# Expert slots without GpSimd arithmetic, weight splits two pieces at a time, and a first slot table that is good for eight slots

## The chip, the cores and the metric

The kernel runs on one core of one Trainium2 chip, which has eight. A core has a matrix engine (PE, TensorE), a vector engine (DVE, VectorE), a scalar engine (ACT, ScalarE), GpSimd (POOL) and SyncE (SP), which here only issues transfers. They run their own instruction streams in order and wait for each other on semaphores. The metric is the device time of one execution in microseconds (us); the lower one is better.

## The reference

The program is an attention with packed keys, a dense two-layer network, and a network of eight experts of which each token takes one:

```
x = attention(q, attention(p, k, v))        # 8 x 8 heads, 576 tokens, width 64; p packs to 32
x: 4608 tokens x 512                         # heads put side by side
h = x @ w_in                                 # 512 -> 2048
g = where(h >= 1, h, where(h <= -1, 0, (h + 1)^2 / 4))
y = g @ w_out                                # 2048 -> 512
logits = y @ w_gate                          # 8 experts
e = argmax(logits); p = softmax(logits)[e]
out = p * (relu(y @ w1[e]) @ w2[e])          # 512 -> 1024 -> 512, the one expert of the token
```

All inputs are float32. With the inputs used, 4594 of the 4608 tokens take expert 2 and 14 take expert 3; the kernel does not know this when it is built.

## The kernel before

**Precision.** Each float32 operand of a product is split in two parts: `hi`, a rounded copy that PE takes at full rate, and `lo = raw - hi`. A product is three matmuls: hi*hi, hi*lo, lo*hi. So each operand costs one copy (on ACT, as a rule) and one subtraction with two inputs in the on-chip memory (on DVE or POOL).

**Stages.** The attention and the packing of the weights take the first stretch. Then the dense network goes through the tokens in 12 tiles of 16 steps (`FC = 16`). A step computes 128 of the 2048 hidden features: the products `h` (L707), the activation on ACT (L729, L730), DVE (L731), ACT (`gh`, L736), DVE or POOL (`gl`, L737), and one step later the products `y` (L712 to L714). Beside tile t + 1 the finished rows of tile t are gated: 24 dot products of a 128x512 block with one expert's gate vector (`jk`, L515, one DVE instruction each with two inputs in the on-chip memory, and one more that reads the sum), then `route` (L517 on: largest logit, place of the token, and an indirect transfer by POOL that sends the row to its expert's list in DRAM). For each pair of blocks these are 8 items of two dots and one `route`.

Then 18 slots of 256 tokens follow, each for one expert, in 8 steps: `gh`, 12 matmuls (L877); `ggh` on ACT (L881) and `ggl` on DVE (L882); `gy`, 6 matmuls (L712 to L714). Last comes a half slot for what is left over. The program is built for any distribution of the tokens, so a **slot table** (`make_table`) is computed on the chip from the counts: which expert each slot takes, from which row on, and whether its weights have to be loaded anew. Table A serves the first `EARLY` slots from the counts known by then, table B the others from all counts. SP reads their entries into registers and issues the loads under a condition.

**Weights of a slot.** Four transfers bring 1 MB each (`raw0` to `raw3`, L825). Each is cut in 128x512 pieces: ACT copies (L860), and `lo_engine` says who subtracts (L861): POOL for all of slots 0 and 1 and half of slot 2, DVE afterwards. All 16 pieces are split for every slot, the weights loaded anew or not. The slot's tokens come as `xb`, are transposed on DVE (L843), copied by ACT (L844), and POOL makes their `lo` part (L845, 128x1024).

**What sets the order.** Everything beside the products is put on a list by step: `at(step, fn)`. Tiles have the steps 0 to 191, slot s starts at `GE + 8*s` with `GE = 192`. Within that, a scheduler at build time orders each engine's instructions, all engines but SP, whose order is that of the program. Tile 11 starts at step `base_a = 176`. Table A takes its counts at `base_a - FC`, that is at the start of tile 10, and is computed from there; the weights of slot 0 are loaded and split beside tile 11. The last tile's gates stand at steps `GE + m//3`, table B at `GE + 8`, and the constants of both tables (`index_tables`) at the start of tile 11.

Of the kernel before, what the change touches and what calls it, by code (L numbers as in the profile page):

```python
# [35 lines left out]
EARLY = 4  # L36
# [48 lines left out]
def attn_moe_kernel(ctx, tc, qT, kT, vv, pT, wcat, wg, w2cat, out):  # L85
# [481 lines left out]
    def index_tables(pl):  # L567


        NM = NMIN - EARLY  # L570
        k = {}
        pi = pl.tile([P, 2], I32, name="pi")
        pool.iota(pi, pattern=[[-1, 2]], base=0, channel_multiplier=1)
        ti = pl.tile([P, 2], I32, name="tail_i")
        dve.tensor_scalar(out=ti, in0=pi, scalar1=-float(NM), scalar2=0.0, op0=ALU.add, op1=ALU.max)
        hi = pl.tile([P, 2, 2], I32, name="half_i")
        dve.tensor_single_scalar(out=hi[:, 0], in_=ti, scalar=1, op=ALU.arith_shift_right)
        dve.tensor_single_scalar(out=hi[:, 1], in_=ti, scalar=1, op=ALU.bitwise_and)
        for n in ("p", "tail", "kf", "off", "cap"):
            k[n] = pl.tile([P, 2], F32, name="k_" + n)  # L580
        hf = pl.tile([P, 2, 2], F32, name="half_f")
        dve.tensor_copy(hf, hi)
        dve.tensor_copy(k["p"], pi)
        dve.tensor_copy(k["kf"], ti)
        dve.tensor_tensor(out=k["kf"], in0=k["p"], in1=k["kf"], op=ALU.subtract)
        dve.tensor_tensor(out=k["kf"], in0=k["kf"], in1=hf[:, 0], op=ALU.add)
        dve.tensor_scalar(out=k["off"], in0=hf[:, 1], scalar1=float(HS), scalar2=None, op0=ALU.mult)
        dve.tensor_scalar(out=k["tail"], in0=k["p"], scalar1=float(NM), scalar2=None, op0=ALU.is_ge)
        dve.tensor_scalar(out=k["cap"], in0=k["tail"], scalar1=float(SL - HS), scalar2=-float(SL), op0=ALU.mult, op1=ALU.add)
        tri8 = pl.tile([P, E, E], F32, name="tri8")  # L590
        pool.memset(tri8, 0.0)
        for e in range(E):
            pool.memset(tri8[:, e, 0:e + 1], 1.0)
        k["tri"] = tri8
        return k

    def make_table(sums, used, nm):
# [5 lines left out]
        k = p3[1]  # L603
# [92 lines left out]
        return ti, un  # L696
# [62 lines left out]
    def evac_tile(t):  # L759
# [198 lines left out]
    for n in range(FC2):  # L958
# [143 lines left out]
```

## Time and profile before

| | |
|---|---|
| three runs | 1266.15, 1267.1, 1267.31 us; median 1267.1 us |
| the profiled execution | 1269.05 us, of which the span of the instructions is 1267.3 us |
| busy share of the span | PE 95%, PEld 79%, DVE 75%, ACT 59%, POOL 33% |
| granted clock of PE, mean | 0.984 |
| tile 10 / tile 11 | 717.29 to 761.29 / 761.29 to 817.90 us |
| slots 0, 1, 2, 3 start at | 817.90, 846.90, 878.27, 904.18 us |
| slots 4 to 16 | 927.65 to 1222.61 us |

A tile's or slot's start is the start of its first product (`h`, L707, or `gh`, L877). PE is the engine that is busy nearly always, so the profile is read for the places where it isn't: how long a stage takes beside what its matmuls need, which wait lies in the gap, and what held the instruction that is waited for.

### The profile page before, as it was taken

What the parts mean: (1) busy time and instruction counts of PE and PEld (TensorE: products, weight loads), DVE (VectorE), ACT (ScalarE), POOL (GpSimd) and SP (SyncE); (2) the same over time, 40 slices, a digit from 0 to 9 for tenths busy, and PEclk for the clock granted to TensorE, in tenths of its full rate; (3) what the DMA queues carried; (4) which work ended last, traced back from release to release, by engine and by line L of the source; (5) the groups of instructions that cost most, each with busy time, mean ns of one, the idle gap of its engine ahead of it and who ended that gap; (6) DMA issues with size and microseconds to landing.
All of it is one profiled execution on the core that took longest, in us unless ns stands there. A gap on an engine that the chain in (4) does not pass through costs nothing.

```text
span 1267.3 us, 21548 instructions
## 1 busy us (share of the span) xinstructions
PE 1199.4 (95%) x7234; PEld 995.6 (79%) x7234; DVE 948.8 (75%) x2296; ACT 741.4 (59%) x1574; POOL 418.5 (33%) x618
## 2 busy tenths in 40 slices
PE   5769999999999999999999998988999999999997
PEld 2446888787788887688888877777899899999996
DVE  7787858988887869969679499798765666666663
ACT  5666656666665566566565556544555565565653
POOL 4230117524730217631113276677212122121210
PEclk8997999999999999999999999899999999999999
DMA  9994870153111232112331005102611212112150
GB/s 343 370 347 152 304 205 22 45 181 114 58 39 44 94 108 76 59 34 67 128 100 33 25 17 179 38 1 68 191 35 42 60 34 68 34 42 60 34 176 21
DMA packets 70183, 128.22 MB, mean 101 GB/s; under 512 B 10281, under 2 KB 46633, under 8 KB 66864
## 3 DMA queue, kind: packets, MB, share of 16 engines
q1 hardware_dynamic: 56464, 97.33, 23.8%
q0 software_dynamic: 5840, 18.95, 3.9%
q10 hardware_dynamic: 7760, 10.49, 2.7%
q8 instruction: 59, 0.97, 0.3%
q14 instruction: 60, 0.49, 0.1%
HBM read 162.31 MB, written 31.77 MB: 153 GB/s over the span
## 4 chain that ended last, share of the span: by engine, by line
PE 71%; DVE 17%; issue 4%; ACT 3%; DMA 3%; POOL 2%; SPq 0%; ACTq 0%; POOLq 0%; DVEq 0%
PE gh L877 14%; PE h L707 13%; PE y L712 8%; PE y L714 8%; PE y L713 8%; DVE jk L515 7%; PE gy L714 5%; PE gy L713 4%; PE gy L712 4%; PE pp L329 2%; DVE rt L731 1%; PE s L215 1%; PE sc L381 1%; PE pp L316 1%; DVE sw L861 1%
## 5 line engine op out<-in xcount | busy, mean ns | idle before, releaser
L707 PE MATMUL h<-ah,pw 128*128 128x256 f32 (+1 forms) x1024 | 243.3, 302 | 8.7 <-DVE rt L731 8.2
L877 PEld LDWEIGHTS gh<-gx,sw 128*128 128x128 f32 x1728 | 230.1, 192 | 14.3
L515 DVE CUSTOM_DVE_ANT_0 jk<-yr,wgb 128x512 bf16<-128x512 f32 x288 | 233.6, 811 | 5.6 <-ACT yr L764 3.5
L877 PE MATMUL gh<-gx,sw 128*128 128x256 f32 x1728 | 233.8, 283 | 0.0
L712 PE MATMUL y<-wo,gh 128*128 128x512 f32 x576 | 230.4, 400 | 0.3 <-ACT kp L391 0.3
L861 DVE TENSOR_TENSOR sw<-raw,sw 128x512 fp32r<-128x512 f32 x264 | 174.5, 710 | 73.1 <-ACT sw L860 73.0
L713 PE MATMUL y<-wo,gh 128*128 128x512 f32 x576 | 228.5, 397 | 0.0
L860 ACT CAST sw<-raw 128x512 fp32r<-128x512 f32 x304 | 169.5, 617 | 63.5 <-PE gy L714 56.1
L707 PEld LDWEIGHTS h<-ah,pw 128*128 128x128 f32 x1024 | 176.9, 190 | 32.7 <-DVE rt L731 14.9
L714 PE MATMUL y<-wo,gl 128*128 128x512 f32 x576 | 186.4, 401 | 2.6 <-POOL gl L737 2.5
L729 ACT ACTIVATE rt<-h,half 128x320 f32<-128x320 f32 (+1 forms) x192 | 111.1, 580 | 99.3 <-PE h L707 80.0
L736 ACT CAST gh<-rt 128x512 fp32r<-128x512 f32 (+2 forms) x192 | 98.2, 512 | 105.7 <-DVE rt L731 59.6
L707 PE MATMUL h<-al,pw 128*128 128x256 f32 (+1 forms) x512 | 152.8, 298 | 0.3 <-POOL al L236 0.3
L731 DVE SCALAR_TENSOR_TENSOR rt<-h,rt 128x320 f32<-128x320 f32 (+1 forms) x192 | 105.3, 550 | 53.2 <-ACT rt L730 48.5
L714 PEld LDWEIGHTS y<-wo,gl 128*128 128x128 f32 x576 | 105.6, 189 | 31.3 <-POOL gl L737 6.5
L712 PEld LDWEIGHTS y<-wo,gh 128*128 128x128 f32 x576 | 108.9, 189 | 25.7 <-issue 3.9
L713 PEld LDWEIGHTS y<-wo,gh 128*128 128x128 f32 x576 | 109.2, 190 | 18.6
L845 POOL TENSOR_TENSOR gx<-xT,gx 128x1024 fp32r<-128x1024 f32 (+1 forms) x19 | 45.6, 2398 | 235.3 <-ACT gx L844 220.2
L712 PE MATMUL gy<-sw,ggh 128*128 128x512 f32 x288 | 113.9, 396 | 0.2 <-ACT ggh L881 0.2
L713 PE MATMUL gy<-sw,ggh 128*128 128x512 f32 x288 | 114.0, 396 | 0.0
L881 ACT ACTIVATE ggh<-gh 128x256 fp32r<-128x256 f32 x144 | 54.9, 381 | 97.7 <-PE gh L877 94.6
L737 DVE TENSOR_TENSOR gl<-rt,gh 128x512 fp32r<-128x512 f32 (+1 forms) x128 | 89.2, 697 | 27.3 <-ACT gh L736 21.9
(220 smaller groups left out, 1827.1 us busy)
## 6 DMA issues: line engine op xcount, KB each, us to landing
raw<-in_w2cat SPq DMA_DIRECT2D x76, 1024.0 KB
ws<-wsd SPq DMA_DIRECT2D x48, 512.0 KB
wr<-in_wcat SPq DMA_DIRECT2D x16, 1024.0 KB
kp<-in_kT SPq DMA_DIRECT2D x16, 576.0 KB
xb<-xs SPq DMA_DIRECT2D x72, 128.0 KB
vr<-in_vv SPq DMA_DIRECT2D x16, 512.0 KB
wsd<-ws SPq DMA_DIRECT2D x8, 1024.0 KB
qr<-in_qT ACTq DMA_DIRECT2D x16, 320.0 KB
```

The source lines that it names most:

```text
L515: dve.tensor_tensor_reduce(out=junk, in0=rows[j][:, :DM], in1=wgb[0][:, e, :], scale=1.0, scalar=0.0, op0=ALU.mult, op1=ALU.add, accum_out ...
L707: pe.matmul(ps[:, col0:col0 + n], lhsT=w[:, g, part, c], rhs=x[:, g, col0:col0 + n], start=(n_mm == 0), stop=(n_mm == 5))
L712: pe.matmul(y, lhsT=gh, rhs=wh, start=first, stop=False)
L713: pe.matmul(y, lhsT=gh, rhs=wl, start=False, stop=False)
L714: pe.matmul(y, lhsT=gl, rhs=wh, start=False, stop=last)
L729: act.activation(v, ps[:, :W], AF.Relu, bias=half, scale=0.5)
L731: dve.scalar_tensor_tensor(out=v, in0=ps[:, :W], scalar=1.0, in1=v, op0=ALU.max, op1=ALU.min)
L736: act.copy(gh[:, :n], vk[:, :n])
L737: (pool if k == "A" else dve).tensor_tensor(out=gl[:, :n], in0=vk[:, :n], in1=f32(gh[:, :n]), op=ALU.subtract)
L860: act.copy(w[:, 0, :], r)
L861: lo_engine(sid, i, n).tensor_tensor(out=w[:, 1, :], in0=r, in1=f32(w[:, 0, :]), op=ALU.subtract)
L877: pe.matmul(ps[:, :SL], lhsT=first(sid, 4 * (fc // 4) + k, part)[:, c], rhs=rh[:, k, :], start=(n_mm == 0), stop=(n_mm == 3 * KD - 1))
```

## The change

- **Who subtracts.** The weight split is called by pair (`m` = 0 to 3) in place of by piece. From slot 1 on, ACT copies and DVE subtracts 128x2x512 in one instruction, and POOL takes none. Slot 0 keeps single pieces; POOL does those of the second layer (`i = 1`, eight), DVE those of the first. The tokens' `lo` part goes from POOL to DVE in two halves of 128x512.
- **The first table.** `EARLY` goes from 4 to 8: table A serves slots 0 to 7 and takes its counts one tile later, at `base_a`. Only three slots' registers are read at once, those of slots 3 to 7 when they are prefetched.
- **The constants** of the tables are made at the program's start.
- **The last tile's gates** stand at steps `GE + 3*m`, and table B is a generator that makes one of ten pieces a step, from `GE + 43` to `GE + 52`.

```diff
-EARLY = 4
+EARLY = 8
...
+    slot_index = index_tables(const)
...
-            at(FC * (t + 1) + (m // 3 if t == NTILE - 1 else min(m, 14 * m // (len(its) - 1))), it)
+            at(FC * (t + 1) + (3 * m if t == NTILE - 1 else min(m, 14 * m // (len(its) - 1))), it)
...
-        pool.tensor_tensor(out=xl[:, :, :W], in0=xT[:, :, :W], in1=f32(xh[:, :, :W]), op=ALU.subtract)
+        for k in range(0, KD, 2):
+            dve.tensor_tensor(out=xl[:, k:k + 2, :W], in0=xT[:, k:k + 2, :W], in1=f32(xh[:, k:k + 2, :W]), op=ALU.subtract)
...
-    def lo_engine(sid, i, n):
-
-        return pool if sid < 2 or (sid == 2 and i == 1) else dve
...
+    def split_w(sid, i, m):
+        w = wtile(f"wo{m}" if i else f"pw1{m}", [P, 2, 2, 512], F32R, f"sw{sid}_{i}_{m}")
+        slot[sid].setdefault("w", {})[i, m] = w
+        for n in (range(2) if sid == 0 else (slice(0, 2),)):
+            r = raw[m][:, n, 512 * i:512 * i + 512]
+            act.copy(w[:, n, 0], r)
+            (pool if sid == 0 and i else dve).tensor_tensor(out=w[:, n, 1], in0=r, in1=f32(w[:, n, 0]), op=ALU.subtract)
...
-        tabA[0], tabA[1] = make_table(sumsA[0], None, "A")
-        for i in range(EARLY):
+        for _ in make_table(sumsA[0], None, "A", tabA):
+            pass
+        for i in range(3):
             slot_regs(i, tabA[0], i, i > 0)
...
-    at(base_a - FC, lambda: sumsA.append(mcum[0]))
+    at(base_a, lambda: sumsA.append(mcum[0]))
...
-    for n in range(FC2):
-        at(base_a + (5, 6, 8, 9, 12, 13, 16, 17)[n], lambda n=n: split_w(0, 0, n))
-        at(base_a + 8 + n, lambda n=n: split_w(0, 1, n))
+    for m in range(4):
+        at(base_a + (6, 9, 13, 17)[m], lambda m=m: split_w(0, 0, m))
+        at(base_a + 9 + 2 * m, lambda m=m: split_w(0, 1, m))
...
-    at(GE + 8, phase_b)
+    for n in range(10):
+        at(GE + 43 + n, phase_b)
...
-        for n in range(FC2):
-            at(b0 + 3 + n, lambda nx=nx, n=n: split_w(nx, 0, n))
-            at(b0 + 2 + n, lambda nx=nx, n=n: split_w(nx, 1, n))
+        for m in range(4):
+            at(b0 + (3, 5, 7, 9)[m], lambda nx=nx, m=m: split_w(nx, 0, m))
+            at(b0 + 2 + 2 * m, lambda nx=nx, m=m: split_w(nx, 1, m))
```

The first place is ACT beside tile 11, from its fifth step's activation (`rt180`) on; `sw0_i_n` is a piece of slot 0's weights of layer `i`. Before:

```order
L729 ACTIVATE rt180_8887<-h11_4_8878,half_94 128x320
L730 ACTIVATE rt180_8887<-rt180_8887 128x320
L729 ACTIVATE rt181_8918<-h11_5_8909,half_94 128x320
L730 ACTIVATE rt181_8918<-rt181_8918 128x320
L736 CAST gh180_8885<-rt180_8887 128x384
L860 CAST sw0_0_0_8936<-raw0_8841 128x512 x2
L860 CAST sw0_1_0_9049<-raw0_8841 128x512 x2
L736 CAST gh181_8916<-rt181_8918 128x384
L729 ACTIVATE rt182_8952<-h11_6_8943,half_94 128x320
L730 ACTIVATE rt182_8952<-rt182_8952 128x320
L860 CAST sw0_1_2_9148<-raw1_8872 128x512 x2
L736 CAST gh182_8950<-rt182_8952 128x384
```

The same place now, five steps further on:

```order
L740 ACTIVATE rt186_9105<-h11_10_9096,half_94 128x320
L741 ACTIVATE rt186_9105<-rt186_9105 128x320
L867 CAST sw0_0_0_8938<-raw0_8814 128x512 x2
L867 CAST sw0_1_0_9086<-raw0_8814 128x512 x2
L747 CAST gh186_9103<-rt186_9105 128x384
L867 CAST sw0_0_1_9091<-raw1_8845 128x512 x2
L867 CAST sw0_1_1_9146<-raw1_8845 128x512 x2
L740 ACTIVATE rt187_9130<-h11_11_9121,half_94 128x320
L740 ACTIVATE rt188_9160<-h11_12_9151,half_94 128x320
L741 ACTIVATE rt187_9130<-rt187_9130 128x320
L867 CAST sw0_0_2_9210<-raw2_8876 128x512 x2
L867 CAST sw0_1_2_9215<-raw2_8876 128x512
```

The first copy of slot 0's weights moved from behind the sixth step's activation to behind the eleventh's, and eight copies stand there within two steps.

The second place is DVE in slot 0, between its third and fourth `ggl` (`ggl0_2`, `ggl0_3`) and on; `jk11_j_e` are the last tile's dots, `sw1` the next slot's weights. Before:

```order
L882 SCALAR_TENSOR_TENSOR ggl0_2_9412<-gh0_2_9398,ggh0_2_9411 128x256
L515 ISA jk11_0_6_9386,L11_0_9316<-yr11_0_9310,wgb_1712 128x512
L515 ISA L11_0_9316 128x1
L515 ISA jk11_0_7_9388,L11_0_9316<-yr11_0_9310,wgb_1712 128x512
...
L882 SCALAR_TENSOR_TENSOR ggl0_3_9486<-gh0_3_9472,ggh0_3_9485 128x256
L515 ISA jk11_1_0_9390,L11_0_9316<-yr11_1_9312,wgb_1712 128x512
...
L532 MAX mx811_0_0_9433<-L11_0_9316 128x8
L515 ISA jk11_1_1_9392,L11_0_9316<-yr11_1_9312,wgb_1712 128x512
```

And now:

```order
L890 SCALAR_TENSOR_TENSOR ggl0_2_9367<-gh0_2_9353,ggh0_2_9366 128x256
L547 ISA jk11_0_6_9584,L11_0_9290<-yr11_0_9284,wgb_1743 128x512
L547 ISA L11_0_9290 128x1
L869 TENSOR_TENSOR sw1_1_0_9377<-raw0_8814,sw1_1_0_9377 128x2x512
L890 SCALAR_TENSOR_TENSOR ggl0_3_9394<-gh0_3_9380,ggh0_3_9393 128x256
L547 ISA jk11_0_7_9586,L11_0_9290<-yr11_0_9284,wgb_1743 128x512
...
L869 TENSOR_TENSOR sw1_0_1_9460<-raw1_8845,sw1_0_1_9460 128x2x512
L890 SCALAR_TENSOR_TENSOR ggl0_4_9424<-gh0_4_9410,ggh0_4_9423 128x256
L547 ISA jk11_1_0_9677,L11_0_9290<-yr11_1_9286,wgb_1743 128x512
```

Between two `ggl` there are now one dot and one subtraction of 128x2x512 where two or three dots stood; the dots of slot 0 are still 16.

## Rows read from the trace of the kernel before

**Rows 1.** Windows by stage: tile 10, tile 11, slots 0 to 3, slots 4 to 16.

```profile
core 0: us, PE busy (x) PEld busy (x) DVE busy (x) ACT busy (x) POOL busy (x), PEclk, DMA share, GB/s
717.29:761.29 44.00, 42.59 (x214) 34.11 (x212) 36.59 (x126) 24.64 (x57) 29.75 (x52) 1.00 0.05 19
761.29:817.90 56.61, 50.57 (x239) 42.19 (x239) 46.39 (x123) 33.28 (x70) 37.23 (x48) 0.94 0.43 122
817.90:927.65 109.75, 98.25 (x594) 85.24 (x593) 92.25 (x211) 53.69 (x112) 60.30 (x45) 0.98 0.24 75
927.65:1222.61 294.96, 294.66 (x1874) 266.56 (x1873) 184.45 (x365) 175.16 (x352) 56.90 (x39) 1.00 0.18 54
```

**Rows 2.** Start, length: products of tile 11's last steps, as one step begins and the next.

```profile
811.94 0.31 PE L707 MATMUL h<-ah,pw 128*128 128x320 f32 x1
...
814.92 0.31 PE L707 MATMUL h<-ah,pw 128*128 128x320 f32 x1
```

**Rows 3.** PE's waits (us in total, times, longest): tile 11, then slots 0 to 3.

```profile
PE h L707 <- DVE rt L731: 3.8, 3, 2.3
PE rk L544 <- DVE M L537: 2.2, 1, 2.2
...
PE gy L714 <- DVE ggl L882: 10.0, 8, 2.1
```

**Rows 4.** Window of ten us behind tile 11's waits.

```profile
790.00:800.00 10.00, 6.25 (x21) 5.21 (x22) 8.22 (x17) 3.34 (x8) 7.14 (x10) 0.71 0.70 104
```

**Rows 5.** Timeline of PE in slot 1.

```profile
852.14 1.11 PE L714 MATMUL gy<-sw,ggl 128*128 128x512 f32 x2 [2.10 <-DVE ggl L882]
```

**Rows 6.** Timeline of DVE: a dot in tile 10; in slot 1 a dot, a `ggl`, a small one.

```profile
753.86 0.68 DVE L515 CUSTOM_DVE_ANT_0 jk<-yr,wgb 128x512 bf16<-128x512 f32 x1
...
848.25 1.81 DVE L515 CUSTOM_DVE_ANT_0 jk<-yr,wgb 128x512 bf16<-128x512 f32 x1
...
851.67 0.41 DVE L882 SCALAR_TENSOR_TENSOR ggl<-gh,ggh 128x256 fp32r<-128x256 f32 x1
...
876.96 3.16 DVE L657 TENSOR_TENSOR eefB<-eefB,eehB 128x2 f32<-128x2 f32 x1
```

**Rows 7.** Timeline of POOL beside slot 1's dots.

```profile
848.23 2.96 POOL L861 TENSOR_TENSOR sw<-raw,sw 128x512 fp32r<-128x512 f32 x2
```

**Rows 8.** Groups by line (busy, mean ns of one, idle before) in slots 0 to 3.

```profile
L861 DVE TENSOR_TENSOR sw<-raw,sw 128x512 fp32r<-128x512 f32 x36 | 29.9, 870 | 7.4 <-ACT sw L860 7.3
L515 DVE CUSTOM_DVE_ANT_0 jk<-yr,wgb 128x512 bf16<-128x512 f32 x24 | 28.8, 1198 | 0.3
...
L861 POOL TENSOR_TENSOR sw<-raw,sw 128x512 fp32r<-128x512 f32 x26 | 38.5, 1508 | 7.3 <-ACT sw L860 7.1
```

**Rows 9.** Groups of the whole run and of slots 4 to 16: pieces, pairs.

```profile
L289 DVE TENSOR_TENSOR ws<-ca,ws 128x1024 fp32r<-128x1024 f32 x8 | 10.1, 1259 | 1.6 <-ACT ws L288 1.6
...
L861 DVE TENSOR_TENSOR sw<-raw,sw 128x512 fp32r<-128x512 f32 x209 | 132.6, 685 | 58.8 <-ACT sw L860 58.8
...
L844 ACT CAST gx<-xT 128x1024 fp32r<-128x1024 f32 x13 | 13.7, 1054 | 0.0
```

**Rows 10.** Timelines of DVE, POOL, SP, ACT: table A and slot 0's weights.

```profile
752.31 0.15 DVE L626 SCALAR_TENSOR_TENSOR cA<-iota,cnA 128x8 f32<-128x8 f32 x1
...
766.82 0.72 POOL L541 TENSOR_TENSOR mcum<-mcum,M 128x8 f16<-128x8 f16 x2 [0.97 <-DVE M L537]
...
767.12 0.16 DVE L689 CAST tiA<-tfA 128x4 int32<-128x4 f32 x1
...
774.44 2.30 SPq L825 DMA_DIRECT2D raw<-in_w2cat  x4
...
779.62 2.19 ACT L860 CAST sw<-raw 128x512 fp32r<-128x512 f32 x4 [1.80 <-DMA raw<-in_w2cat]
...
783.97 1.14 ACT L860 CAST sw<-raw 128x512 fp32r<-128x512 f32 x2 [0.82 <-DMA raw<-in_w2cat]
```

**Rows 11.** Timeline of DVE in the first stretch.

```profile
7.70 0.76 DVE L388 TENSOR_REDUCE nm<-sc 128x1 f32<-128x576 f32 x1 [2.96 <-PE sc L381]
```

More of the change, by code (lines that the diff above doesn't have):

```diff
@@ L127, in attn_moe_kernel, with index_tables @@
                 pool.iota(tokid[:, t, j:j + 1], pattern=[[0, 1]], base=t0 + tile_start(t) + c - (HB if tile_kind(t) == "B" else 0), channel_multiplier=1)
+    def index_tables(pl):
+        NM = NMIN - EARLY
+        k = {}
+        pi = pl.tile([P, 2], I32, name="pi")
+        pool.iota(pi, pattern=[[-1, 2]], base=0, channel_multiplier=1)
+        ti = pl.tile([P, 2], I32, name="tail_i")
+        dve.tensor_scalar(out=ti, in0=pi, scalar1=-float(NM), scalar2=0.0, op0=ALU.add, op1=ALU.max)
+        hi = pl.tile([P, 2, 2], I32, name="half_i")
+        dve.tensor_single_scalar(out=hi[:, 0], in_=ti, scalar=1, op=ALU.arith_shift_right)
+        dve.tensor_single_scalar(out=hi[:, 1], in_=ti, scalar=1, op=ALU.bitwise_and)
+        for n in ("p", "tail", "kf", "off", "cap"):
+            k[n] = pl.tile([P, 2], F32, name="k_" + n)
+        hf = pl.tile([P, 2, 2], F32, name="half_f")
+        dve.tensor_copy(hf, hi)
+        dve.tensor_copy(k["p"], pi)
+        dve.tensor_copy(k["kf"], ti)
+        dve.tensor_tensor(out=k["kf"], in0=k["p"], in1=k["kf"], op=ALU.subtract)
+        dve.tensor_tensor(out=k["kf"], in0=k["kf"], in1=hf[:, 0], op=ALU.add)
+        dve.tensor_scalar(out=k["off"], in0=hf[:, 1], scalar1=float(HS), scalar2=None, op0=ALU.mult)
+        dve.tensor_scalar(out=k["tail"], in0=k["p"], scalar1=float(NM), scalar2=None, op0=ALU.is_ge)
+        dve.tensor_scalar(out=k["cap"], in0=k["tail"], scalar1=float(SL - HS), scalar2=-float(SL), op0=ALU.mult, op1=ALU.add)
+        tri8 = pl.tile([P, E, E], F32, name="tri8")
+        pool.memset(tri8, 0.0)
+        for e in range(E):
+            pool.memset(tri8[:, e, 0:e + 1], 1.0)
+        k["tri"] = tri8
+        return k
+    slot_index = index_tables(const)
     packed = st2.tile([P, 2 * B, D], F32, name="packed")
@@ L565, in gate_items, with make_table @@
         return items
[L567 to L603, printed above, removed]
+    def make_table(sums, used, nm, out_tab):
+        k = slot_index
         def t(shape, dt, n):
@@ L638, in make_table @@
         if used is not None:
+            yield
             nh = t([P, E], F32, "nh")
@@ L666, in make_table @@
         dot(c, oh, 1)
+        yield
         j = t([P, 1], F32, "j")
@@ L695, in make_table @@
             dve.scalar_tensor_tensor(out=un, in0=Sf, scalar=float(EARLY), in1=un, op0=ALU.min, op1=ALU.subtract)
-        return ti, un
+        out_tab.extend((ti, un))
     def ffn1(t, fc, ps):
@@ L957, in attn_moe_kernel, with phase_b @@
     at(base_a + 13, lambda: slot_x(0))
[L958 to L960 removed]
+    for m in range(4):
+        at(base_a + (6, 9, 13, 17)[m], lambda m=m: split_w(0, 0, m))
+        at(base_a + 9 + 2 * m, lambda m=m: split_w(0, 1, m))
     nact = [None]
[L964 to L966 removed]
+    def phase_b(box=[]):
+        if not box:
+            box.append(make_table(mcum[0], tabA[1], "B", tabB))
+        next(box[0], None)
     def count_slots():
         nact[0] = nc.values_load(tabB[0][0:1, 3:4], min_val=0, max_val=NTAIL, skip_runtime_bounds_check_because="halves left of NT tokens")
[L971 removed]
     at(GE + FC2 * (NMIN - 2), count_slots)
[L973 removed]
+    for n in range(10):
+        at(GE + 43 + n, phase_b)
     def regs_for(sid):
[L976 removed]
+        if 2 < sid < EARLY:
+            slot_regs(sid, tabA[0], sid, True)
+        elif sid >= EARLY:
             slot_regs(sid, tabB[0], sid - EARLY, sid > EARLY, SL if sid < NMIN else HS)
@@ L1049, in attn_moe_kernel @@
                 slot_x(sid)
-                for n in range(FC2):
-                    split_w(sid, 0, n)
-                    split_w(sid, 1, n)
+                for m in range(4):
+                    split_w(sid, 0, m)
+                    split_w(sid, 1, m)
             half_slot(sid)
```

26 lines of the change are left out of this document (9 added, 17 removed).

## The prediction, made before the changed kernel ran

> **What bounds the kernel now.** I read the windows by stage first, to see where PE is not full. Slots 4 to 16 take 294.96 us and PE is busy 294.66 of them [rows 1]: 22.69 us a slot, the products alone. Slots 0 to 3 run the same products and take 109.75, which is 18.99 over 4 x 22.69. Tile 11's last `y` products fall behind slot 0's first product; nine of 512 columns beside six of 320 are 0.71 of a step, and a step without a wait takes 814.92 - 811.94 = 2.98 us [rows 2], so 2.1 of the 18.99 are work. 16.9 us are lost. Tile 11 needs 16 x 2.98 = 47.7 and takes 56.61: 8.9 lost.
>
> The second view is PE's list of waits. In tile 11, 3.8 us stand with `rt` and 2.2 with `M` [rows 3], 6.0 in all. The rest is the clock: in the ten us behind these waits, in which PE was busy for 6.25, the granted clock is 0.71 [rows 4], so nearly six of ten at the lower of the two levels (1.2 in place of 2.4 GHz), about 2.9 lost; 6.0 + 2.9 = 8.9. In slots 0 to 3 10.0 of the lost 16.9 stand with `ggl`, eight times [rows 3].
>
> The third is DVE's timeline ahead of such a wait. PE begins at 852.14 after 2.10 us for `ggl` [rows 5]; that `ggl` takes 0.41, begins at 851.67 and stands behind two dots, of which the first took 1.81 [rows 6]. A dot in tile 10 took 0.68. POOL ran its splits beside the slow ones [rows 7]. Over the four slots 24 dots mean 1198 ns, POOL's 26 splits 1508 [rows 8]; and a subtraction of two columns took 3.16 [rows 6]. So DVE instructions with two inputs in the on-chip memory and POOL's splits lengthen each other, and DVE, busy 92.25 of 109.75 [rows 1], delivers `ggl` late.
>
> **Slots 0 to 3.** POOL's 26 splits go. The 24 dots return to about 0.69: 24 x (1.198 - 0.69) = 12.2 us of DVE time. All splits then are DVE's: 62 pieces are 31 pairs. A pair is not in the trace as such; the nearest rows are the 128x1024 subtraction, 1259 ns, and two pieces at 2 x 685 = 1370 [rows 9]. I take the first, the same element count in one instruction: 31 x 1.26 = 39.1 in place of 29.9 [rows 8], 9.2 more. The tokens' `lo`, 4 x 2 halves at 0.69, is 5.5 more. DVE comes to 92.25 - 12.2 + 9.2 + 5.5 = 94.7, and would fill the 4 x 22.69 + 2.1 = 92.9 us if nothing else left it. But what is left of the 92.25 beside dots, splits and 32 `ggl` at 0.41, 92.25 - 28.8 - 29.9 - 13.1 = 20.5 [rows 1, 6, 8], holds table B, which moves two slots on, and the time for which small instructions were held (3.16 for one). I take 8 of it as gone, an estimate between 3 (the held ones alone) and 13. So 86.7 of 92.9, 93%, tight but under. Slot 0 is the tightest: between `ggl0_0` and `ggl0_7` the order has 15 dots, 6 pairs, 7 `ggl`: 15 x 0.69 + 6 x 1.26 + 7 x 0.41 = 20.8 us, where seven steps of the floor are 7/8 x 22.69 = 19.9. A loss of 1.0 there, and 1.5 in the three others, remain: 16.9 - 2.5 = **14.4 us gained**. Bounds: 16.9 if DVE is never late, 9.4 if the `ggl` waits keep half their length too (5.0 on top of the 2.5).
>
> **Tile 10.** Table A's 45 or so small DVE instructions leave it for tile 11. PE is idle for 44.00 - 42.59 = 1.4 us in it [rows 1]; I take 1.0 back, between 0 and 1.4.
>
> **Tile 11.** Its counts now include tile 9, which POOL has added up at 766.82 + 0.72 = 767.5, where before the first table instruction stood at 752.31 [rows 10]. From there to the last (767.12) are 14.8 us; from that to SP's first load of weights 7.3, in which registers of four slots, 11 values, are read; from the load to ACT's first copy, which waited for it 1.80, 5.2. In the changed order: 767.5 + 14.8 = 782.3, 8 values of 11 make 5.3, so the load at 787.6, and the first MB at 792.8. Less tile 10's 1.0, 791.8. ACT comes to that copy behind the eleventh step's activation: 760.3 + 10 x 2.98 + about 1.5 = 791.6. So ACT waits little for the first transfer, but the copies from the second began 783.97 - 779.62 = 4.35 behind those from the first, and after a wait [rows 10], so the second MB lands at about 796. Four pieces (2.19) are done by 794, and a `gh` follows, so ACT waits about 1.7 for the second MB, and I take 1.8 for the two others together. ACT's work in the last five steps (14.9 us): 16 copies at 0.55 = 8.8, and the activation, 1.54 a step as in tile 10 (24.64 / 16 [rows 1]), 7.7; with 3.5 of waits 20.0. That is 5.1 over, of which I take 1.2 as hidden (the activation stands less than half a step ahead of its use), so PE loses about 3.9. What was lost before (8.9) goes, since nothing of slot 0 stands with ACT before the eleventh step and the dots of tile 10 meet no POOL split: 8.9 - 3.9 = 5.0. For a short fall of the clock I take off 0.4: **4.6 us gained**. Bounds: 8.9 if the loads are in time; -0.9 if they are 3 us later and the clock falls for as long as before (3.9 + 3.0 + 2.9 = 9.8).
>
> The Trainium skill, "SBUF — State Buffer", § Who interferes with whom, says that a DVE instruction with two inputs there and a GpSimd one that reads there exclude each other for a whole instruction. The rows agree in kind: 1.81 against 0.68. By that rule the eight splits that slot 0 leaves with POOL may each hold DVE for a whole 1.5 us, 12 us beside the last five steps, and if PE waited for a third of it 4 us of the gain would be missing; by the rows it is less, since beside POOL's 38.5 us of splits in slots 0 to 3 the dots lost only 12.2.
>
> **The rest.** Slots 4 to 17: pairs are cheaper for ACT (1.05 by the 128x1024 copy [rows 9]), DVE has 8 x 1.26 + 2 x 0.69 + 8 x 0.41 and the transposes in 22.69, and it was busy only 184.45 of 294.96 [rows 1]. Nothing, between -0.3 and +1; the work that hides a pair is a step of PE, 2.84, and one `ggl` may be late in the last slot, where no prefetch follows: +0.3 (0 to 1). The constants, eleven small DVE instructions, fit in a gap of 2.96 us that ends at 7.70 [rows 11]: 0 to 0.4, I take 0.1. The eight-slot table moves an unconditional load of weights from slot 4 to slot 8, and slot 4's cost no wait that PE's list shows: 0.
>
> Sum: -14.4 - 1.0 - 4.6 + 0.3 + 0.1 = -19.6. The profiled execution took 1269.05, so 1249.45; it was 1.95 above the runs' median, so **1247.5 us**.
>
> **Rivals.** *Slot 0's weights are late.* ACT takes its work in order, and a copy that waits holds the activation behind it; if four copies wait as above and PE's clock falls once more, tile 11 keeps its 56.6 and 4.6 are missing: 1252.1. For it: ACT waited 1.80 and 0.82 with a load that was issued 13 us earlier [rows 10]; against: the copies now stand five steps later. Chance 0.2.
>
> *DVE is full.* It takes POOL's part, and is at 93% by my sum. If slots 0 to 3 give back 9.4 in place of 14.4: 1252.5, and with DVE's other bound (8 taken as 3, so 5 more) up to 1257.5. For: the 20.8 against 19.9 in slot 0; against: it sat idle 7.4 before its splits, nearly all for ACT's copies [rows 8]. Chance 0.13.
>
> *The pairs delay `ggl` in every slot* (the other side). A pair is 1.26 on DVE and 1.05 on ACT, and where two stand ahead of a `ggl` both engines hand it over later. In seventeen slots a loss of 1.15 a slot (19.6 / 17) eats the gain; one pair's length too late once a slot, 1.26 x 17 = 21.4, would give 1268.9, and twice 1290. Against it: DVE is idle for 37% of slots 4 to 16 and a `ggl` is used one step later. Chance 0.04.
>
> *It is not DVE.* If `ggl` were late by ACT and the dots slow by themselves, slots 0 to 3 would keep their length: 1247.5 + 14.4 = 1261.9. The dot of 0.68 speaks against. Chance 0.03.
>
> **Chances.** The forecast has the other 0.6, with a range of its own of 1243 to 1252. With the first two rivals, 0.93, the range is **1242 to 1256**: below, all bounds at their best would be 1240. Less than 0.2% (2.5 us) can't be told from no change here: faster 0.95, within 0.01, slower 0.04.
>
> **What the profile after would show.** Right: dots at 0.69 in slots 0 to 3, none above 1; no `ggl` wait over 0.6; slots 0 to 3 together 95 to 96 us; tile 11 about 52 with waits only in its last five steps, behind ACT's copies; later slots at 22.7. Wrong: a slot after 4 over 22.9; a wait for weights above 3 us at once; the clock under 0.9 in tile 11; or DVE busy over 97% in slots 0 to 3 with PE waiting for `ggl`.

## The result, and the profile after

The changed kernel takes 1249.1 us (median of four runs, 1248.49 to 1249.28) against 1267.2 before in the same comparison: a ratio of 0.9855, 95% interval 0.9839 to 0.9871. The forecast was 1247.5, 1242 to 1256. The profiled execution took 1249.28, its span is 1247.3.

By stage, as in [rows 1] (the window, its length, busy PE, PEld, DVE, ACT, POOL, the granted clock, DMA), tile 10, tile 11, slots 0 to 3, slots 4 to 16:

```profile
719.38:762.47 43.09, 41.46 (x213) 33.95 (x211) 35.87 (x103) 24.98 (x58) 28.48 (x42) 1.00 0.05 19
762.47:813.96 51.49, 49.01 (x239) 41.08 (x240) 44.41 (x142) 33.19 (x70) 26.41 (x39) 0.97 0.43 123
...
813.96:908.64 94.68, 93.88 (x594) 84.34 (x593) 79.57 (x214) 51.28 (x81) 13.55 (x17) 1.00 0.17 48
908.64:1203.31 294.67, 294.67 (x1874) 267.03 (x1872) 192.15 (x287) 166.91 (x248) 25.29 (x26) 1.00 0.23 68
```

| stage | before | after | difference | forecast |
|---|---|---|---|---|
| up to the first tile | 62.65 | 64.12 | +1.5 | +0.1 |
| tiles 0 to 9 | 654.64 | 655.26 | +0.6 | 0 |
| tile 10 | 44.00 | 43.09 | -0.9 | -1.0 |
| tile 11 | 56.61 | 51.49 | -5.1 | -4.6 |
| slots 0 to 3 | 109.75 | 94.68 | -15.1 | -14.4 |
| slots 4 to 16 | 294.96 | 294.67 | -0.3 | 0 |
| slot 17 to the end of the span | 44.69 | 43.99 | -0.7 | +0.3 |
| sum (spans) | 1267.3 | 1247.3 | -20.0 | -19.6 |

In slots 0 to 3 PE is busy 93.88 of 94.68 us; the ten us of waits for `ggl` [rows 3] are gone, and its list of waits from tile 11's first product on has these two rows left (us in all, times, longest), the first at and in tile 11, the second in the slots:

```profile
PE h L718 <- DVE rt L742: 3.6, 3, 2.0
...
PE rk L577 <- POOL mcum L573: 0.8, 1, 0.8
```

The groups of DVE in slots 0 to 3 (busy, mean ns of one, idle before) answer to [rows 8]: a dot takes 686 ns where it took 1198, the 30 pairs and one single piece 37.0 us together (the pairs alone have a mean of 1220 ns), and the group of POOL's splits does not exist any more.

```profile
L869 DVE TENSOR_TENSOR sw<-raw,sw 128x1024 fp32r<-128x1024 f32 (+1 forms) x31 | 37.0, 1204 | 7.5 <-ACT sw L867 7.4
L547 DVE CUSTOM_DVE_ANT_0 jk<-yr,wgb 128x512 bf16<-128x512 f32 x24 | 16.5, 686 | 0.2
```

**The first stretch** lost what was not foreseen. DVE's timeline, where it waited 2.96 us for PE before [rows 11], and POOL's timeline beside it:

```profile
6.21 3.26 DVE L137 TENSOR_SCALAR tail_i<-pi 128x2 int32<-128x2 int32 x1 [1.57 <-POOL pi L135]
6.28 3.19 DVE L145 CAST k_p<-pi 128x2 f32<-128x2 int32 x1
9.50 0.56 DVE L139 TENSOR_SCALAR half_i<-tail_i 128x2 int32<-128x2 int32 x1
...
10.62 0.74 DVE L420 TENSOR_REDUCE nm<-sc 128x1 f32<-128x576 f32 x1
```

```profile
6.45 2.24 POOL L455 MEMSET pk<- 128x2560 f32 x1
8.62 0.53 POOL L456 MEMSET pkf<- 128x512 f32 x1
9.08 0.36 POOL L155 MEMSET tri<- 128x1 f32 x8
```

Two constants of two columns take 3.2 us each: they begin within 0.3 us of POOL's large memset and end as the last memset ends. The first softmax maximum, which PE's products had released at 7.70 before, comes at 10.62.

**Tile 11** in four timelines: ACT's copies of slot 0's weights with what they waited for, then DVE, POOL and PE where the longest wait stands.

```profile
794.55 2.18 ACT L867 CAST sw<-raw 128x512 fp32r<-128x512 f32 x4 [1.19 <-DMA raw<-in_w2cat]
...
803.90 1.14 ACT L867 CAST sw<-raw 128x512 fp32r<-128x512 f32 x2 [0.56 <-DMA raw<-in_w2cat]
```

```profile
801.04 2.75 DVE L869 TENSOR_TENSOR sw<-raw,sw 128x512 fp32r<-128x512 f32 x2
803.71 0.48 DVE L742 SCALAR_TENSOR_TENSOR rt<-h,rt 128x320 f32<-128x320 f32 x1
```

```profile
799.84 7.89 POOL L869 TENSOR_TENSOR sw<-raw,sw 128x512 fp32r<-128x512 f32 x5
```

```profile
762.47 0.41 PE L718 MATMUL h<-ah,pw 128*128 128x320 f32 x1 [1.16 <-DVE rt L742]
...
804.24 0.41 PE L718 MATMUL h<-ah,pw 128*128 128x320 f32 x1 [2.02 <-DVE rt L742]
```

ACT waited 1.75 us for weights, half of what was forecast (3.5). PE has two waits inside the tile, 0.46 and 2.02. The wait of 2.02 ends with an `rt` that stood behind two pieces of 2.75 us together, 1.38 each, and POOL was splitting for 7.89 us beside them. The weights' load, on SP's timeline, was issued at 789.60:

```profile
789.60 2.37 SPq L836 DMA_DIRECT2D raw<-in_w2cat  x4
```

The wait of 1.16 lies ahead of the tile's first product, so it counts for tile 10. The `rt` that ends it stood behind several dots, of which one took 2.42 us beside GpSimd's subtractions for the dense tile (`gl`, 128x256), which the change left with GpSimd. DVE's row, then two of POOL's:

```profile
758.11 2.42 DVE L547 CUSTOM_DVE_ANT_0 jk<-yr,wgb 128x512 bf16<-128x512 f32 x1
```

```profile
758.39 0.73 POOL L748 TENSOR_TENSOR gl<-rt,gh 128x256 fp32r<-128x256 f32 x1
...
759.26 0.72 POOL L748 TENSOR_TENSOR gl<-rt,gh 128x256 fp32r<-128x256 f32 x1
```

### The profile page after: what moved, and what is told of

Read it like the earlier page. It is cut to its first block, busy times and chain, and to the rows that moved or that the text cites. A ratio compares the mean times of both kernels' runs of the same rounds, so it can differ in the third digit from the quotient of the medians.

```text
span 1247.3 us, 21251 instructions
## 1 busy us (share of the span) xinstructions
PE 1193.9 (96%) x7234; PEld 995.3 (80%) x7234; DVE 944.6 (76%) x2222; ACT 730.0 (59%) x1430; POOL 325.5 (26%) x567
## 5 line engine op out<-in xcount | busy, mean ns | idle before, releaser
L869 DVE TENSOR_TENSOR sw<-raw,sw 128x1024 fp32r<-128x1024 f32 (+1 forms) x152 | 180.9, 1209 | 77.9 <-ACT sw L867 77.8
L885 PEld LDWEIGHTS gh<-gx,sw 128*128 128x128 f32 x1728 | 227.1, 191 | 12.8
L885 PE MATMUL gh<-gx,sw 128*128 128x256 f32 x1728 | 230.5, 283 | 0.0
L547 DVE CUSTOM_DVE_ANT_0 jk<-yr,wgb 128x512 bf16<-128x512 f32 x288 | 219.1, 761 | 5.6 <-ACT yr L775 3.5
L718 PEld LDWEIGHTS h<-ah,pw 128*128 128x128 f32 x1024 | 176.5, 190 | 31.0 <-DVE rt L742 13.4
L867 ACT CAST sw<-raw 128x1024 fp32r<-128x1024 f32 (+1 forms) x160 | 156.5, 1004 | 59.1 <-PE gy L725 53.9
L908 POOL DMA_INDIRECT out<-go,xm x37 | 36.8, 993 | 362.3 <-ACT go L907 303.1
L748 DVE TENSOR_TENSOR gl<-rt,gh 128x512 fp32r<-128x512 f32 (+1 forms) x128 | 84.1, 658 | 25.3 <-ACT gh L747 21.2
```

The source lines that it names most:

```text
L547: dve.tensor_tensor_reduce(out=junk, in0=rows[j][:, :DM], in1=wgb[0][:, e, :], scale=1.0, scalar=0.0, op0=ALU.mult, op1=ALU.add, accum_out ...
L718: pe.matmul(ps[:, col0:col0 + n], lhsT=w[:, g, part, c], rhs=x[:, g, col0:col0 + n], start=(n_mm == 0), stop=(n_mm == 5))
L748: (pool if k == "A" else dve).tensor_tensor(out=gl[:, :n], in0=vk[:, :n], in1=f32(gh[:, :n]), op=ALU.subtract)
L867: act.copy(w[:, n, 0], r)
L869: (pool if sid == 0 and i else dve).tensor_tensor(out=w[:, n, 1], in0=r, in1=f32(w[:, n, 0]), op=ALU.subtract)
L885: pe.matmul(ps[:, :SL], lhsT=first(sid, 4 * (fc // 4) + k, part)[:, c], rhs=rh[:, k, :], start=(n_mm == 0), stop=(n_mm == 3 * KD - 1))
```

## The experiments

All are variants of the changed kernel except the second. The table has the stages of each profile (us; the starts as before), the median, and the ratio to the kernel before on the same chip with its interval. The chips of the three groups differ a little, so variants are compared by ratio or by stage.

| kernel | first tile at | tile 10 | tile 11 | slots 0-3 | median | ratio |
|---|---|---|---|---|---|---|
| e1 GpSimd back in the slots | 64.34 | 43.09 | 51.75 | 113.78 | 1268.78 | 1.0000 (0.9989-1.0011) |
| e2 before, splits moved only | 62.12 | 43.83 | 55.02 | 94.52 | 1251.39 | 0.9870 (0.9850-0.9891) |
| e3 single pieces | 64.07 | 43.03 | 52.95 | 94.47 | 1250.36 | 0.9863 (0.9843-0.9883) |
| e4 constants late | 62.61 | 43.49 | 51.09 | 94.69 | 1249.91 | 0.9856 (0.9840-0.9872) |
| e5 changed kernel again | 65.24 | 43.03 | 51.51 | 94.69 | 1250.15 | 0.9866 (0.9848-0.9885) |
| e6 slot 0 on DVE | 63.58 | 43.14 | 50.41 | 94.74 | 1248.65 | 0.9851 (0.9834-0.9869) |
| e7 table early | 64.06 | 42.71 | 52.39 | 94.71 | 1250.17 | 0.9869 (0.9847-0.9891) |
| e8 constants first | 62.51 | 43.03 | 51.51 | 94.68 | 1247.31 | 0.9840 (0.9822-0.9859) |
| e9 = e6 + e8 | 62.78 | 42.94 | 50.71 | 94.68 | 1245.60 | 0.9825 (0.9809-0.9841) |
| e10 = e9, gates close | 62.88 | 43.01 | 50.75 | 94.79 | 1246.78 | 0.9835 (0.9818-0.9851) |
| e11 = e9 + e7 | 63.31 | 42.72 | 49.83 | 94.72 | 1248.13 | 0.9850 (0.9833-0.9866) |
| e12 memsets on GpSimd | 63.64 | 43.04 | 51.38 | 95.24 | 1250.01 | one run |

**e1: GpSimd takes its part of the slots again.**

```diff
-        for n in (range(2) if sid == 0 else (slice(0, 2),)):
+        gp = sid in (1, 2) and (sid == 1 or i == 1) or sid == 0 and i
+        for n in (range(2) if sid == 0 or gp else (slice(0, 2),)):
...
-            (pool if sid == 0 and i else dve).tensor_tensor(out=w[:, n, 1], ...)
+            (pool if gp else dve).tensor_tensor(out=w[:, n, 1], ...)
...
+        pool.tensor_tensor(out=xl[:, :, :W], in0=xT[:, :, :W], ...)    # in place of two halves on dve
```

> The changed kernel, with GpSimd taking again what it took in the slots: the splits of slots 1 and half of slot 2 in single pieces, and the tokens' lo part in one instruction; table, gates, pairs for the other slots as in the changed kernel. Theory (GpSimd and the vector engine hold each other up): slots 0 to 3 go from 94.7 back towards 109.75, to 105 to 110 us, the dots from 686 ns to over 1000, and the time to 1259 to 1265. Rival (pairs, or the gates and table B spread over later steps, brought it): slots 0 to 3 stay under 99 and the time under 1254.

Measured: the whole gain is gone (ratio 1.0000), slots 0 to 3 take 113.78. The window, the groups of DVE and of POOL there, and PE's waits:

```profile
816.80:930.58 113.78, 102.03 (x594) 90.70 (x593) 90.52 (x199) 53.31 (x94) 59.84 (x44) 0.93 0.14 40
```

```profile
L547 DVE CUSTOM_DVE_ANT_0 jk<-yr,wgb 128x512 bf16<-128x512 f32 x24 | 27.4, 1141 | 0.3
...
L688 DVE TENSOR_TENSOR jB<-jB,vvB 128x1 f32<-128x1 f32 x1 | 3.0, 2993 | 0.0
```

```profile
L869 POOL TENSOR_TENSOR sw<-raw,sw 128x512 fp32r<-128x512 f32 x24 | 35.2, 1495 | 15.1 <-ACT sw L867 15.0
L856 POOL TENSOR_TENSOR gx<-xT,gx 128x1024 fp32r<-128x1024 f32 x4 | 11.2, 2795 | 9.2 <-ACT gx L855 9.2
```

```profile
PE gy L725 <- DVE ggl L890: 6.9, 3, 2.6
PE rk L576 <- DVE M L569: 4.9, 1, 4.9
```

The dots are back at 1141 ns, with DVE busy no more than 90.52 of 113.78 us by its records. Late table, spread gates and pairs in the other slots kept nothing: it is GpSimd's presence, not DVE's load, that costs the slots their time. Slots and time came out some 4 us above the ranges expected, and the slots 4 us above the kernel before. That difference is in PE's busy time, the same 594 matmuls: 102.03 us at a granted clock of 0.93, where the kernel before has 98.25 at 0.98 [rows 1]; PE's idle time is nearly the same, 11.8 and 11.5 us.

**e2: the kernel before with that part alone.**

```diff
-        pool.tensor_tensor(out=xl[:, :, :W], in0=xT[:, :, :W], in1=f32(xh[:, :, :W]), op=ALU.subtract)
+        for k in range(0, KD, 2):
+            dve.tensor_tensor(out=xl[:, k:k + 2, :W], in0=xT[:, k:k + 2, :W], ...)
...
-        return pool if sid < 2 or (sid == 2 and i == 1) else dve
+        return pool if sid == 0 and i else dve
```

> The kernel before with that one part of the change: GpSimd keeps the second layer of slot 0's weights and gives all other splits and the tokens' lo part to the vector engine, in single pieces; old table, gates and constants. Theory: slots 0 to 3 come to 95 to 97 us although table B is still computed in them and the dots stand close, because the dots return to 0.69 us; tile 11 to 52 to 53; time 1248 to 1252, so all of the change's gain or more. Rival (the spread of the gates and of table B is needed, as the vector engine is over 93% full): slots 0 to 3 at 100 to 104 and the time 1255 to 1260.

Tile 11, then slots 0 to 3:

```profile
760.48:815.50 55.02, 50.19 (x238) 41.81 (x239) 47.10 (x135) 34.83 (x72) 26.48 (x42) 0.94 0.44 125
815.50:910.02 94.52, 94.35 (x594) 84.19 (x593) 80.34 (x241) 52.53 (x109) 11.21 (x13) 1.00 0.27 87
```

94.52 us, as short as in the changed kernel, though the gates stand close. Table B is computed in these slots too; by the trace that is so in the changed kernel as well, whose scheduler draws it forward (below). DVE is busy for 80.34. The time is 1251.39; tile 11 came to 55.0, not 52 to 53, some 3 us more than in the changed kernel, at a granted clock of 0.94. That the earlier table and weights cost it is not shown: e7 has them early as well and takes 52.39.

**e3: single pieces.**

```diff
-        for n in (range(2) if sid == 0 else (slice(0, 2),)):
+        for n in range(2):
```

> The changed kernel with the splits of all slots in single pieces of 128x512, everything else as it is. By the traces a pair costs 1.20 us and two pieces 2 x 0.69 = 1.38 on the vector engine, so slots 0 to 3 need 31 x 0.18 = 5.6 us more of it in 94.7, of which 79.6 are busy. Theory: no wait of TensorE comes of it: the time within 1 us of 1249.1, the last slot a little shorter (a piece stands ahead of its ggl in place of a pair). Rival (the pairs carry a part of the gain): slots 0 to 3 at 97 to 100, the time 1252 to 1255.

Slots 0 to 3 take 94.47, the ratio is that of the changed kernel within its interval: the pairs brought nothing that could be seen, and they cost no `ggl` in these slots either. The median is 1.3 us above 1249.1, on another chip, where 1 was expected at most. Tile 11, which the edit leaves as it is, took 52.95 at a granted clock of 0.94 in this profile; the changed kernel has 0.97 there.

**e4 and e8: where the constants are made.** e4 makes them at the start of tile 11, as before the change; e8 moves the block of `index_tables` and its call ahead of the loop over `tokid`.

```diff
-    slot_index = index_tables(const)          # e4
+    slot_index = {}
...
+        slot_index.update(index_tables(p3[0]))   # in open_p3
```

> The changed kernel with the constants of the tables made where the kernel before made them, at the start of tile 11. Theory (the small vector instructions at the start are held behind GpSimd's memset of 128x2560, so the first softmax maximum comes 2.9 us late): the first tile starts 1.5 to 2.1 us earlier (62.0 to 62.7), tile 10 no longer than 43.8, the time 1247.0 to 1248.0. Rival (the first stretch differs from run to run by that much anyway): the first tile starts at 63.5 to 64.5 again and the time is within 0.7 us of 1249.1.

> The changed kernel with the constants of the tables made ahead of the token numbers, so that GpSimd's part stands some 4 us earlier than its memset of 128x2560. Theory: the small vector instructions are done before 5 us, the first softmax maximum comes at 7.7 to 8.2 in place of 10.6, the first tile starts at 62.0 to 63.0, and the time falls by 1 to 2 us against the changed kernel on this chip. Rival (what follows absorbs it): the maximum is early but the first tile starts at 63.5 or later.

DVE's timeline in e8:

```profile
2.25 0.17 DVE L126 TENSOR_SCALAR tail_i<-pi 128x2 int32<-128x2 int32 x1 [0.55 <-POOL pi L124]
...
7.96 0.76 DVE L420 TENSOR_REDUCE nm<-sc 128x1 f32<-128x576 f32 x1 [2.88 <-PE sc L413]
```

The same constant takes 0.17 in place of 3.26, and the maximum comes at 7.96. (In e8 GpSimd runs short iotas and small memsets beside the constants.) Over all profiles the first tile starts at 63.58 to 65.24 in the seven with the constants between (mean 64.15) and at 62.12 to 63.31 in the seven with them elsewhere (mean 62.69): 1.5 us, without overlap. e8 ran 2.8 us under the changed kernel on its chip (e5), whose first stretch was the longest of all. In e4 the first tile starts as early, but its median did not fall, against the expectation; the executions of one kernel differ by 1 to 4 us (in e1 by 6), so in times e4 is inconclusive. Its profile (span 1245.5) speaks for the gain, but that execution was the shortest of five.

**e6: slot 0 without GpSimd as well.**

```diff
-            (pool if sid == 0 and i else dve).tensor_tensor(out=w[:, n, 1], ...)
+            dve.tensor_tensor(out=w[:, n, 1], ...)
```

> The changed kernel with the last eight splits of GpSimd, the second layer of slot 0's weights, on the vector engine too. Theory (what is left of tile 11's loss is again the two engines holding each other: pieces of 1.2 to 1.4 us on the vector engine where one alone takes 0.69, ahead of the rt that TensorE waits for): tile 11 goes from 51.5 to 48.5 to 50, the time down by 1.3 to 3 us. Rival (the weights come too late, ACT waits for them): tile 11 stays at 51 or gets longer, since the vector engine has 8 x 0.69 = 5.5 us more to do in its last five steps.

Tile 11's window, and two rows of DVE's timeline in it:

```profile
762.13:812.55 50.42, 47.73 (x240) 39.89 (x241) 43.85 (x149) 33.12 (x70) 13.07 (x30) 1.00 0.44 126
```

```profile
797.77 2.53 DVE L869 TENSOR_TENSOR sw<-raw,sw 128x512 fp32r<-128x512 f32 x4
...
800.72 1.89 DVE L869 TENSOR_TENSOR sw<-raw,sw 128x512 fp32r<-128x512 f32 x3
```

Four pieces take 2.53 where two took 2.75. DVE has eight splits more and is busy no longer (43.85 against 44.41). Tile 11 gets 1.1 us shorter and the wait of 2.02 is 0.5, but waits of 1.2 and 1.1 for `gh` and `gl` stand there now. PE's idle time in the tile is no less, 2.7 us (50.42 - 47.73) against 2.5 (51.49 - 49.01); what fell in this profile is PE's busy time, at a granted clock of 1.00 in place of 0.97. In e9, which has the same edit and 0.97, it is the idle time that fell, to 1.7:

```profile
759.70:810.42 50.72, 49.00 (x240) 41.29 (x241) 44.19 (x149) 33.14 (x70) 13.70 (x30) 0.97 0.44 126
```

By stage the three kernels with this edit and the late table (e6, e9, e10) take 50.41 to 50.75 us, and those with the late table and GpSimd's splits 51.09 to 51.75 (52.95 in e3). So both expectations hold a part: of the 3.8 us that tile 11 lost, about 1 was GpSimd's, the rest is not, and how that 1 divides between waits and clock isn't settled.

**e7: the weights earlier.**

```diff
-EARLY = 8
+EARLY = 6
...
-    at(base_a, lambda: sumsA.append(mcum[0]))
+    at(base_a - FC, lambda: sumsA.append(mcum[0]))
```

with the gates at `2 * m` and table B from `GE + 29`.

> The changed kernel with table A computed a tile earlier, as before the change, but good for 6 slots (EARLY = 6), the last tile's gates at every second step and table B from step GE + 29 on; GpSimd keeps its eight splits of slot 0. Theory of late weights (the rival that the prediction named): ACT never waits for weights, the copies spread over the whole tile, tile 11 at 48 to 49.5, the time 2 to 3 us down. Theory of the two engines holding each other: the splits meet the dots of tile 10 now, tile 11 stays at 51 to 53 and the time does not fall.

ACT's copies stand 15 us earlier, and a dot of tile 10 beside GpSimd's splits is slow (timelines of ACT, DVE and POOL):

```profile
779.02 2.19 ACT L867 CAST sw<-raw 128x512 fp32r<-128x512 f32 x4 [2.69 <-DMA raw<-in_w2cat]
...
783.16 1.14 ACT L867 CAST sw<-raw 128x512 fp32r<-128x512 f32 x2 [1.58 <-DMA raw<-in_w2cat]
```

```profile
780.89 1.76 DVE L547 CUSTOM_DVE_ANT_0 jk<-yr,wgb 128x512 bf16<-128x512 f32 x1
```

```profile
780.78 6.23 POOL L869 TENSOR_TENSOR sw<-raw,sw 128x512 fp32r<-128x512 f32 x4 [2.41 <-ACT sw L867]
```

ACT waits longer for its weights there, 4.27 us in all, since the scheduler puts the copies as early as the load. So the edit did not take away the wait that the theory of late weights speaks of, and tile 11's 52.39 us do not refute that theory. They fit the other one: the splits meet the dots of tile 10, and the time does not fall.

**e5, e9, e10, e11: the same again, and what adds up.** e5 is the changed kernel unchanged. e9 has e6 and e8 together; e10 puts e9's gates back to `m // 3`; e11 is e9 with e7's table.

> The changed kernel once more, as the measure for the three that follow on the same chip. Its profiles' stages: first tile at 64.1, tile 10 43.1, tile 11 51.5, slots 0 to 3 94.7 us. If the first stretch is the program's and not chance, the first tile starts at 64.0 to 64.4 once more.

> The changed kernel with both mended terms: constants ahead of the token numbers, and slot 0's second layer on the vector engine. The two gains lie in different stages (first stretch 1.5 to 2 us, tile 11 1.1 us), so they should add: 2.6 to 4 us under the changed kernel, first tile at 62.0 to 63.0, tile 11 at 50 to 50.8. If GpSimd's splits were only a symptom in tile 11, nothing beyond the constants' part.

> The kernel with both mended terms, and the last tile's gates back at steps GE + m//3, as before the change; table B stays late. Theory (without GpSimd the vector engine has room, and the scheduler draws 16 of the dots into slot 0 either way): slots 0 to 3 at 94 to 95 us, time within 0.7 us. Rival (spreading the gates was needed): slots 0 to 3 at 97 or more, time 2 us or more above the other.

> Both mended terms, and table A a tile earlier and good for 6 slots, with the gates at every second step and table B from GE + 29 on. With no GpSimd split in tile 11 the early weights can pay: tile 11 at 48 to 49.5 (floor 47.7), 1 to 2.5 us under the kernel with the two mended terms. If the vector engine's own load sets tile 11 (dots of tile 10, eight splits more), it stays at 50 or above.

e5's first tile starts at 65.24, not at 64.0 to 64.4: one kernel's first stretch differs by 1.1 us between two profiles. e9 takes 1245.60, ratio 0.9825: the best of all, 17.5 per mille under the kernel before where the changed kernel has 13.4 to 14.5. Its two gains stand in their stages (first tile 62.78, tile 11 50.71). e10's slots take 94.79: the spread of the gates bought nothing there, and the intervals of e9 and e10 overlap. e11's tile 11 is 49.83, 0.9 shorter than e9's, where 48 to 49.5 was expected; but its granted clock is 1.00 there and e9's 0.97, and e6, at 1.00, has 50.41. So a gain from early weights is not shown. The time is not better either (1248.13, expected 1 to 2.5 under e9). That stays open.

**e12: GpSimd writes, but does not read.** In slots 0 and 1, behind each `ggh`:

```diff
+        if sid < 2:
+            act.copy(scr[0][:, 0:1], f32(gh[:, 0:1]))
+            for _ in range(3):
+                pool.memset(scr[0], 0.0)
```

> The changed kernel with work added to GpSimd that reads nothing: in slots 0 and 1, behind every ggh, three memsets of 128x512 into a tile of their own, tied to the step by a small copy on ACT (0.2 us). If it takes a GpSimd instruction that reads to hold a dot up, the dots stay at 0.69 us and slots 0 to 3 under 96; if any GpSimd access to the memory does it, the dots beside memsets take 0.9 us or more and slots 0 and 1 lose several us.

DVE's dots and GpSimd's memsets in slots 0 and 1, by group; below them a dot and a memset at the same time:

```profile
L547 DVE CUSTOM_DVE_ANT_0 jk<-yr,wgb 128x512 bf16<-128x512 f32 x24 | 16.4, 685 | 0.2
```

```profile
L898 POOL MEMSET scr<- 128x512 f32 x45 | 23.7, 526 | 16.5 <-ACT scr L896 14.9
```

```profile
821.52 0.68 DVE L547 CUSTOM_DVE_ANT_0 jk<-yr,wgb 128x512 bf16<-128x512 f32 x1
```

```profile
821.90 0.53 POOL L898 MEMSET scr<- 128x512 f32 x1 [1.14 <-ACT scr L896]
```

45 memsets, 23.7 us in 48, leave the dots at 685 ns and slots 0 to 3 at 95.24. A GpSimd memset, which only writes, holds no dot up; the subtractions of the slots before, which read two operands, did. One that reads a single operand was not tried. The Trainium skill, "SBUF — State Buffer", § Who interferes with whom, says the same of a two-input instruction beside a GpSimd write. It also says that `cast` and `tensor_scalar` can take both ports and then contend with GpSimd, if their operands meet certain conditions. The 3.26 us at the start fit that; whether that instruction took both ports no run here shows.

## Why the prediction was right, and where it was not

**Slots 0 to 3** (forecast -14.4, measured -15.1). The mechanism was right and is shown from both sides: e1 brings the loss back with everything else changed, e2 takes it away with nothing else changed. The sum's parts were less exact. Of the 15.1 us, 10.7 are PE's idle time (11.50 before, 0.80 after) and 4.4 its busy time: the same 594 matmuls took 98.25 us at a granted clock of 0.98 and take 93.88 at 1.00. The prediction named only the waits for `ggl`, 10.0 of its 16.9; the clock's share came back without being a term. The dots at 0.69 were right (686 ns). DVE's load was put at 86.7 us and is 79.57: a pair takes 1.22, not 1.26, and of the 20.5 us of other instructions about 12.5 went, not 8. Table B, which was to move two slots on, is not among them. The change calls it from slot 5 on, but the scheduler drew it forward, and its last instruction stands in these four slots after as before:

```profile
883.46 0.17 DVE L700 CAST tiB<-tfB 128x4 int32<-128x4 f32 x1
```

```profile
888.74 0.13 DVE L689 CAST tiB<-tfB 128x4 int32<-128x4 f32 x1
```

So what went was for the most part time for which small instructions were held beside GpSimd: the one of two columns that took 3.16 [rows 6] takes 0.15. So the rival "DVE is full" had the wrong idea of the load: what looked like work in DVE's 92.25 us [rows 1] was partly waiting that is booked as busy.

**Tile 11** (-4.6, measured -5.1). Right in size, only partly in reason, so the size is luck in part. The forecast left a loss of 4.3 us, 3.9 by ACT's wait for late weights and its copies and 0.4 by the clock. Counted from the tile's start, the load was issued at 27.1 and the first copy began at 32.1 us, close to what was worked out (26.3 and 31.5), but ACT waited 1.75, not 3.5. The tile lost 3.8 us: PE's two waits are 2.5, and its clock about 1.3 (busy for 49.01 us at 0.97, where e6 has 47.73 at 1.00). The longer wait, 2.02, came from DVE's pieces beside GpSimd's eight splits and not from ACT's copies. That is the place where the prediction weighed the rule of mutual exclusion and decided for less: e6, e9 and e10 give about 1 us for those eight splits, between the nothing of the sum and the 4 that the paragraph on the rule gave.

**Tile 10** (-1.0, measured -0.9). Right in size, but not for the reason given, that table A's instructions leave it. In e7 and e11 they are back in tile 10 (from 753.6 on in e7), and it takes 42.71 and 42.72 us. It takes 43.5 to 44.0 in the three kernels whose trace has the constants in it (before, e2, and e4 at 743.2), and 42.7 to 43.1 in all others: the gain goes with the constants. Nor did PE's idle time fall, from which the 1.0 was taken: 1.41 us before, 1.63 after (43.09 - 41.46). So this was luck.

**The first stretch** is the step that failed: eleven small DVE instructions that "fit in a gap of 2.96 us", 0 to 0.4. Each was priced at its duration alone, and what POOL did in that gap was not weighed; a memset of 2.24 us stood there before the change too:

```profile
6.29 2.24 POOL L423 MEMSET pk<- 128x2560 f32 x1
```

Measured 1.5 us at the first tile, by e8 and by all fourteen profiles. The +0.6 of tiles 0 to 9 isn't settled: in e8 these tiles take 655.07 us, hardly less than the 655.26 here, so it is not the constants; e5, the same kernel once more, has 654.99, so it may be scatter.

**Later slots and the end.** Steady slots lost nothing, so the rival of late pairs falls (e3 as well). From slot 17 to ACT's last instruction the time grew by 0.3, as forecast. After, then before:

```profile
1241.47 0.69 ACT L907 ACTIVATE go<-gy,xm 128x512 f32<-128x512 f32 x1 [5.29 <-PE gy L725]
```

```profile
1260.45 0.69 ACT L899 ACTIVATE go<-gy,xm 128x512 f32<-128x512 f32 x1 [5.31 <-PE gy L714]
```

(1241.47 - 1203.31 = 38.16; before 1260.45 - 1222.61 = 37.84.) The pairs are the cause: with single pieces, in e3, it is 37.90. From there to the end of the span, with the last transfer, it took 5.9 us where it took 6.8, which the sum did not have. This goes with GpSimd as well: it is 6.8 in the two kernels in which GpSimd makes the tokens' `lo` part (before, e1), 5.9 in eleven others and 6.2 in e12 with its memsets. Why, no run shows.

**From profile to median.** The sum gave 1249.45 for the profiled execution, and that took 1249.28. The 1.95 that were then taken off, since the profiled execution of before stood that far above its median, did not come back: after, it stands 0.2 above. An execution's excess is scatter of that execution (runs of the kernel before lay between 1265.23 and 1272.34 in all comparisons; the profiled one of e1 stands 3.3 above its median, that of e4 2.4 below) and nothing here lets it carry over to another kernel. This is the whole miss of 1.6 us.

**The other parts of the change.** Pairs: nothing (e3), but for the 0.3 that they cost in the last slot. Gates spread: nothing in the slots (e10). Table later: no gain from bringing it back (e7, e11); against e2 tile 11 is 3.5 us shorter, for which no single part has been shown to be the cause. Constants early: 1.5 us lost in the first stretch, and some of tile 10's 0.9 won. So 15 of the 20 us between the profiles hang on who subtracts. e2, which changes that alone, runs 16.6 us under its before, the changed kernel 18.1 and in e5 17.5, and the intervals of the ratios overlap: that the rest of the change gives anything is not shown by the times.

## What to carry to other kernels

A helper engine that takes work off a full one can cost more than it takes: look at the same instruction's duration with and without the helper beside it (0.68 against 1.81 here) before counting the helper's work as saved. Moving instructions into a gap of one engine needs a look at what the other engines do to the memory in that gap. And a profile's time that lies above the median of its runs is not to be subtracted from a forecast. Last, a stage that comes out at its forecast length proves the reason only if a run tests it: tile 10's 0.9 us stayed when the part that was to give it was put back.

## What the hardware showed unexpectedly

- A `tensor_scalar` of two columns, one input, took 3.26 us beside GpSimd's memsets of 2.24 and 0.53 us, and 0.17 beside its short iotas and memsets in e8, while a two-input dot of 512 columns beside memsets kept its 0.685 (e12) and went to 1.14 beside GpSimd subtractions (e1). So here it was the pair of instructions that counted, not their size.
- One DVE subtraction of 128x2x512 takes 1.22 us where two of 128x512 take 1.37 [rows 9]; eight of them a slot are a saving that no one waits for.
